# Fixed order of the first loads, and a new order of all other work, in a planned adaLN + linear attention + SwiGLU kernel

## Chip, cores and metric

The kernel runs on one core of one Trainium2 chip. The metric is device time in microseconds (us), as the median of several executions. One execution is also taken by the hardware profiler; the span is the time from its first to its last instruction.

The engines are called PE (matmuls; PEld is its weight load), DVE (vector), ACT (activations), POOL (GpSimd) and SP, which here only issues DMAs.

## The reference

The input x has 2048 tokens of 512 values in bf16. A row `c` gives six modulation vectors. Then come an attention block with feature maps (32 heads of 16), and a gated feed-forward block of width 1376:

```python
mod = (silu(c) @ w_mod).reshape(1, 6, 1, -1)        # sa, ca, ga, sb, cb, gb
h = layernorm(x) * (1 + ca) + sa
x = x + ga * A(h)
h = layernorm(x) * (1 + cb) + sb
x = x + gb * ((silu(h @ w_gate) * (h @ w_up)) @ w_down)

def A(h):                                           # per head
    q, k, v = split(h @ wqkv)
    phi(t) = concat(softmax(t @ w_phi), softmax(-t @ w_phi))
    kv = phi(k).T @ v ;  z = sum over tokens of phi(k)
    return (phi(q) @ kv / (phi(q) @ z + 1e-6)) @ wo
```

## The kernel before

**Tiles and stages.** The 2048 tokens are 16 tiles of 128, in four chunks (`x_ch`, 512 tokens each). The stages are these:

- The first norm: `bn_stats` (L345), `bn_aggr` (L346), the reciprocal root on ACT (L374, L375) or POOL (L378, L379), the negated product with the mean (L381), and normalization to `xn` (L389 on DVE, L393 on ACT, L395 on POOL).
- The modulation: `silu(c)` as a column, then 8 columns of `w_mod` times it for each of 4 row blocks k (L468). Scale and shift of the first norm go to `modA` (L473, L474).
- The fold of `w_phi` into the key and query weights. The 128-row blocks of the weights are transposed (key weights on PE, L515 and L519; query weights by DMA, L292), multiplied with a block-diagonal `BD` made from `w_phi` (L495, L498), by L526, and written back (L529 on ACT, L530 on DVE).
- The turn of `xn` into `hT` (features on partitions). Chunk 0 and the start of chunk 1 go through PE (L558, L411), and ACT or DVE evacuate them with scale and shift (L565, L567, L419, L422). Later tiles go through DMA transposes (L579) with L589 on ACT or L591 on POOL.
- For every tile a key product (L622), exponentials of both signs (L633), their sums S (L639), reciprocals (L643, L644), a value product (L626) scaled into `va` (L649), and the sum over tokens in `kv_ps` (L662). Query tiles do the like with L685, L689, L693 to L700 and a DMA transpose `pT` (L704).
- Attention outputs: L805, reciprocal `A` (L808), `o` (L809), turned by DMA into `oT` (L828) or on PE (L824), projected with `wo` (L838), added to x (L841). `wo` has been scaled by the gate before, on POOL (L761).
- The second norm and the feed-forward block: L890 and L930 (gate and up), L897 to L906, L962 (down), L973, L977, and the stores (L982).

**What sets the order.** Every piece of work is recorded as an `Op` with its alternatives (the engines that could do it and their planned durations), what it reads and what it writes. A list `ORDER`, written out in the file (L47 to L86), then names the operations one by one: `x // 4` is the number of the operation, `x % 4` the chosen alternative. `Plan.run` goes through it and gives each operation a planned start, from the engine's planned free time, the planned ends of what it reads, and the planned landing of DMAs. The instructions are issued in the order of the planned starts. So `ORDER`, and also the planned durations and the constant `DMA`, decide how instructions stand in each engine's queue; the engines then run their queues in order.

```python
            if o.eng == "XBAR" and o.kb > 0:
                dma = max(dma, o.start + self.DMA[0]) + o.kb * 1024 / self.DMA[1]
                o.end = max(o.end, dma + self.DMA[2])
```

**Loads.** All loads are issued by SP (`later`, L289), and the transposes by DMA as well (`transposed`, L292; L579, L704, L828, L852, L942). The row `c` alone comes through ACT's queue. The second argument of `Buf(at=...)` is a planned time before which a buffer counts as not there (`bc` is the row `c`).

**Fill.** Where the plan leaves PE idle, `fill` (its matmul is L1029) puts matmuls on a tile of ones in front of the operation that comes next, by the length of the planned gap, up to 90 us.

Of the kernel before, what the change touches and what calls it, by code (L numbers as in the profile page):

```python
# [35 lines left out]
def fm_size(m):  # L36
# [7 lines left out]


ORDER = [
    20, 44, 0, 48, 8, 56, 4, 64, 148, 12, 52, 264, 272, 116, 164, 24, 268, 276, 16, 168, 280, 172, 76, 176, 68, 181, 284, 290, 80, 72, 152, 294, 60,  # L47
    100, 120, 132, 136, 196, 200, 184, 156, 32, 84, 105, 88, 94, 124, 108, 189, 160, 140, 312, 98, 204, 144, 194, 320, 208, 240, 212, 113, 296, 36,
    28, 245, 316, 128, 324, 304, 248, 216, 228, 548, 224, 301, 329, 233, 364, 480, 332, 376, 252, 220, 464, 420, 236, 308, 472, 512, 424, 338, 257,
    468, 432, 756, 261, 40, 368, 552, 456, 760, 428, 484, 437, 342, 476, 372, 516, 520, 460, 400, 440, 388, 380, 444, 792, 588, 556, 384, 489, 404,  # L50
    592, 452, 448, 392, 852, 860, 800, 492, 408, 502, 524, 344, 396, 628, 498, 354, 816, 856, 506, 358, 560, 529, 808, 536, 636, 532, 565, 584, 724,
    362, 804, 412, 416, 660, 544, 820, 728, 928, 796, 732, 632, 812, 600, 572, 540, 350, 596, 1064, 764, 624, 668, 956, 568, 824, 768, 605, 1072,
    960, 510, 580, 932, 964, 828, 664, 576, 773, 838, 608, 612, 968, 640, 780, 833, 1300, 644, 1068, 845, 1276, 1316, 616, 992, 996, 620, 864, 841,
    784, 869, 848, 648, 776, 938, 972, 950, 1280, 946, 941, 1004, 892, 1009, 976, 788, 872, 888, 900, 876, 1012, 984, 1000, 1160, 896, 980, 988,
    1076, 1200, 952, 1164, 880, 1304, 1016, 904, 884, 736, 1204, 909, 1240, 1172, 1285, 1024, 652, 1177, 912, 916, 1244, 1298, 1212, 1028, 1324,
    1248, 1168, 1332, 1208, 921, 740, 1184, 1289, 924, 1196, 1180, 1294, 1217, 1328, 656, 1020, 1189, 1192, 1312, 1220, 744, 1232, 1492, 1236, 692,
    1252, 1320, 1257, 1260, 748, 1272, 1496, 1224, 1229, 1336, 1264, 1341, 1344, 1268, 1572, 1576, 1356, 1080, 1532, 1084, 1504, 1360, 1536, 1509,
    1512, 1348, 1584, 1544, 1612, 1616, 1500, 1516, 1589, 1524, 1528, 1624, 1353, 1308, 696, 1549, 1580, 1540, 1556, 1592, 1521, 1596, 1629, 1561,
    1652, 700, 1620, 1604, 1568, 1601, 752, 1608, 1636, 1552, 1641, 1396, 1564, 1632, 1644, 1088, 1788, 1648, 1400, 1796, 1780, 1800, 1128, 1136,
    1404, 704, 1804, 1808, 1716, 1656, 1828, 672, 1832, 1784, 1660, 1032, 1724, 1836, 1748, 1840, 1408, 2288, 1428, 2292, 708, 2296, 1792, 712, 716,  # L60
    1720, 1412, 1844, 1848, 1092, 1040, 676, 1852, 1856, 1860, 1036, 2300, 1436, 1752, 1044, 1132, 2452, 680, 2456, 720, 684, 1864, 1048, 2460,
    1756, 1052, 1684, 1460, 1432, 1468, 1056, 1096, 2304, 1464, 1869, 1104, 1880, 1872, 1364, 688, 2308, 1884, 1060, 1816, 1877, 2312, 2136, 2140,
    2316, 1692, 1100, 1368, 1944, 2320, 1416, 2144, 1892, 1108, 1112, 1688, 1372, 1888, 2326, 1924, 1932, 1928, 2148, 1908, 2328, 2440, 1116, 1140,
    1916, 2444, 1912, 1144, 1936, 2152, 1948, 2448, 1984, 1120, 1920, 1940, 2156, 1148, 2346, 1896, 1988, 1960, 1952, 2341, 1900, 1964, 1992, 2160,
    2164, 1996, 1124, 2334, 1824, 2337, 2168, 2174, 1956, 2000, 1376, 2348, 1420, 2404, 2464, 2400, 1472, 2352, 2692, 2004, 2380, 2408, 1904, 1968,
    2008, 2388, 2356, 2176, 2492, 1152, 2364, 1380, 2012, 2412, 2368, 2372, 2016, 2496, 2468, 1476, 2020, 2025, 1384, 2500, 2384, 2189, 1156, 1424,
    1480, 2036, 1388, 2696, 2360, 2182, 2504, 2193, 2376, 1972, 2186, 2392, 2028, 2700, 1392, 2416, 2508, 2396, 2472, 2040, 2704, 2196, 2032, 2248,
    2252, 2228, 1664, 2708, 2476, 2712, 2256, 2044, 2480, 2236, 1440, 1484, 2484, 2490, 2096, 2956, 2200, 2100, 2204, 2960, 1668, 2716, 1672, 1444,
    2048, 2420, 2424, 1448, 1676, 2052, 2964, 1696, 1452, 2104, 2232, 1488, 2944, 2513, 2948, 2260, 2240, 2212, 2744, 2428, 2076, 2516, 2080, 1680,
    1456, 2952, 3208, 2720, 1976, 2244, 2748, 1760, 2526, 2968, 2752, 1700, 2084, 3212, 1704, 1708, 1764, 3216, 2108, 2521, 2533, 2529, 2756, 2216,  # L70
    2724, 2088, 2536, 1768, 1772, 2540, 2060, 2760, 2092, 3196, 1728, 2612, 3200, 2576, 1732, 2068, 2728, 3204, 2064, 2220, 2732, 2996, 2056, 1736,
    3448, 2584, 2628, 2208, 2765, 2224, 2972, 2620, 2072, 2556, 3452, 1776, 2736, 2742, 3000, 3456, 3712, 2976, 2608, 1712, 2264, 3004, 3220, 1740,
    2616, 2980, 3008, 3716, 3248, 2984, 3012, 3720, 3252, 3460, 2636, 2988, 3224, 3256, 2564, 2268, 3017, 2993, 2272, 2572, 2624, 2544, 2768, 3464,
    3228, 2548, 1744, 2774, 2786, 3468, 3260, 2780, 2777, 2560, 3264, 3700, 3232, 2788, 2792, 3020, 2796, 2580, 2568, 3472, 3704, 3236, 2592, 3708,
    3034, 2112, 3026, 3030, 3724, 3240, 3269, 3037, 2800, 2596, 3245, 2600, 3040, 3044, 3476, 3480, 2116, 3048, 3484, 3488, 2120, 2588, 3272, 2276,
    3500, 3052, 2552, 3504, 3492, 1980, 3728, 2124, 2860, 2432, 3290, 3752, 3508, 3732, 3278, 3512, 2808, 3736, 3281, 2604, 3516, 3740, 3496, 3756,
    2632, 3285, 3760, 3292, 2816, 3744, 3521, 3056, 3764, 3768, 3749, 3296, 2644, 2640, 2844, 2812, 2820, 3773, 3524, 2648, 3776, 3542, 2652, 2824,
    2852, 2864, 3530, 3533, 2804, 2656, 3537, 2281, 3794, 2832, 2872, 3544, 3786, 3548, 2848, 3060, 2668, 2672, 2856, 3789, 3552, 2284, 2868, 3782,
    3068, 3796, 2676, 3800, 2828, 3064, 2876, 3804, 3808, 3300, 2836, 2840, 3812, 2884, 2680, 3072, 2880, 2888, 2892, 3304, 3832, 2896, 3836, 2661,
    2436, 3872, 3844, 3880, 2900, 3840, 3308, 2920, 2685, 2904, 3816, 3824, 3848, 2924, 2928, 3820, 3852, 3828, 3888, 3896, 2932, 2688, 3928, 2908,  # L80
    3868, 3892, 2912, 3856, 3876, 2937, 3116, 3860, 3884, 3864, 3900, 3556, 2940, 3076, 3932, 3936, 3124, 3112, 3084, 2128, 3120, 3132, 3140, 3128,
    3136, 3080, 3088, 3092, 3940, 3144, 3096, 3100, 3332, 3172, 3148, 3104, 3108, 3176, 3180, 3152, 3156, 3184, 3340, 3620, 1812, 3384, 3328, 2664,
    3616, 3904, 3628, 3560, 3624, 3160, 2132, 3945, 3312, 3189, 3908, 2916, 3336, 3320, 3632, 3912, 3192, 3344, 3165, 3316, 3364, 3916, 3920, 3348,
    3372, 3368, 3352, 3376, 3324, 3400, 3584, 3356, 3360, 3948, 3424, 3392, 3388, 3380, 3396, 3404, 3428, 3924, 3408, 3412, 3592, 3564, 3432, 3580,
    3436, 3588, 3600, 3168, 1821, 3568, 3572, 3608, 3640, 3636, 3596, 3604, 3440, 3576, 3652, 3644, 3444, 3676, 3612, 3416, 3420, 3648, 3656, 3660,
    3664, 3680, 3669, 3684, 3688, 3693, 3672, 3696, 3952, 3956, 3960, 3964, 3968,  # L86
]


# [32 lines left out]
class Plan:  # L122
# [1 line left out]

    HOP = {"PE": 0.24, "DVE": 0.2, "ACT": 0.2, "POOL": 0.14, "SP": 0.0, "XBAR": 0.08, "NONE": 0.0}
    OWN = {"PE": 0.0, "DVE": 0.19, "ACT": 0.19, "POOL": 0.12, "SP": 0.0, "XBAR": 0.0, "NONE": 0.0}
    DMA = (1.9, 385e3, 0.5, 0.7, 1.3, 1.0)
    LANES = 8

    def __init__(self, slots):  # L130
# [37 lines left out]
    def run(self, fill):  # L168
# [3 lines left out]
        for x in ORDER:  # L172
# [16 lines left out]
# [3 lines that stand above are left out]
            elif o.eng == "XBAR" and o.kb == 0:  # L192
                dma = max(dma, o.end + 0.1) + self.DMA[4 if o.alt[1] > 1.32 else 3]
                o.end = max(o.end, dma + self.DMA[5])
            elif o.kb < 0:
# [13 lines left out]
def kernel(  # L209
# [125 lines left out]
    bwo = [Buf() for _ in range(KD)]  # L335
    bwd = [Buf() for _ in range(FM)]
    bwgu = [Buf(), Buf()]
    bc, bphi = Buf(at=2.75), Buf()
    bWq2 = [Buf() for _ in range(KD)]
    bWk2 = [Buf() for _ in range(KD)]  # L340

# [727 lines left out]
```

## Time and profile before

| what | value |
|---|---|
| median of 5 runs | 202.76 us |
| lowest, highest | 202.27, 203.21 us |
| time of the profiled execution | 202.27 us |
| its span | 200.5 us |
| mean granted TensorE clock | 0.997 |
| PE, DVE, ACT, POOL busy | 193.7, 137.3, 110.1, 125.1 us |

Busy time is the union of an engine's instructions, and its share is of the span. PE's instructions overlap in its pipeline, and its busy time counts the fill as well. 24 matmuls of the kernel are fill. A line in the fences below that begins with a time is a group of like instructions that follow one another: start, length, engine, line, operation, tiles written and read. Square brackets give the idle time of that engine just before, and what ended it.

### The profile page before, as it was taken

The page shows a single profiled execution, that of the slowest core. Times are in us where ns is not written, and L with a number is a line of the kernel's source. Part 1 is how long each engine was busy: PE and PEld are TensorE (multiplying, and loading weights), DVE is VectorE, ACT ScalarE, POOL GpSimd, SP SyncE. Part 2 cuts the span into 40 slices and gives each one's busy share as a digit, 9 for nine tenths or more (in the row PEclk, how much of TensorE's full clock was granted, in tenths as well). Part 3 has the DMA queues.
Part 4 walks back from the last instruction along what each step waited for, and adds up shares of the span by engine and source line. Part 5 has one row for each costly group of instructions (what it writes and reads, how often), then busy time and mean ns, then how long its engine had stood idle before and what let it go on. Part 6 is the DMA issues. An engine that isn't in the chain of part 4 may idle for free.

```text
span 200.5 us, 4670 instructions
## 1 busy us (share of the span) xinstructions
PE 193.7 (97%) x1767; PEld 131.4 (66%) x1767; DVE 137.3 (68%) x277; ACT 110.1 (55%) x244; POOL 125.1 (62%) x211
## 2 busy tenths in 40 slices
PE   7799999999999989999999999999999999999993
PEld 2474555555564767788876767678668867686852
DVE  5979999999989989999988839523314314122343
ACT  2589999998679973571635444562413431341310
POOL 3473999999998997889795758472016260440510
PEclk9999999999999999999999999999999999999998
DMA  5997997989633663949767551721001002010012
GB/s 170 342 351 163 247 310 183 300 157 355 219 56 72 128 97 78 118 94 148 147 129 136 105 105 52 77 70 37 18 26 54 3 7 86 12 56 0 0 56 67
DMA packets 51081, 24.22 MB, mean 121 GB/s; under 512 B 42257, under 2 KB 47858, under 8 KB 51058
## 3 DMA queue, kind: packets, MB, share of 16 engines
q1 hardware_dynamic: 50912, 23.85, 51.6%
q8 instruction: 14, 0.23, 0.5%
q10 hardware_dynamic: 146, 0.07, 0.1%
q14 instruction: 9, 0.07, 0.1%
HBM read 11.58 MB, written 2.10 MB: 68 GB/s over the span
## 4 chain that ended last, share of the span: by engine, by line
PE 84%; ACT 6%; DMA 5%; DVE 2%; SPq 1%; issue 1%; ACTq 0%; DVEq 0%
PE one_ps L890 34%; PE one_ps L962 18%; PE one_ps L626 7%; PE one_ps L838 6%; PE one_ps L622 5%; PE one_ps L685 5%; DMA wmod_sb<-in_w_mod_dram 3%; ACT eq L689 3%; PE one_ps L930 3%; PE kv_ps L662 2%; DMA oT<-o 2%; PE kv_ps L805 2%; PE one_ps L717 1%; PE one_ps L526 1%; SPq L289 1%; ACT hT L565 1%
## 5 line engine op out<-in xcount | busy, mean ns | idle before, releaser
L890 PE MATMUL one_ps<-hT,wgu_sb 128*128 128x256 bf16 (+1 forms) x800 | 76.9, 251 | 0.0
L890 PEld LDWEIGHTS <-wgu_sb 128*128 128x128 bf16 x800 | 65.6, 98 | 10.7
L897 ACT ACTIVATE sg<-one_ps 128x512 bf16<-128x512 f32 (+1 forms) x42 | 23.2, 575 | 39.5 <-PE one_ps L890 32.9
L962 PE MATMUL one_ps<-wd_sb,gu 128*128 128x512 bf16 (+2 forms) x176 | 40.9, 372 | 0.0
L906 POOL TENSOR_TENSOR gu<-usb,sg 128x512 bf16<-128x512 bf16 x16 | 18.4, 1153 | 32.2 <-ACT sg L897 24.5
L900 DVE TENSOR_TENSOR gu<-one_ps,sg 128x512 bf16<-128x512 f32 (+1 forms) x26 | 16.5, 640 | 29.5 <-PE one_ps L890 23.1
L962 PEld LDWEIGHTS <-gu 128*128 128x128 bf16 (+1 forms) x187 | 18.1, 98 | 15.3
L973 DVE TENSOR_TENSOR fg<-one_ps,gab 128x512 bf16<-128x512 f32 (+1 forms) x16 | 10.6, 668 | 15.8 <-PE one_ps L962 15.8
L345 DVE BATCH_NORM_STATS2 st<-x_c 128x6 f32<-128x512 bf16 x32 | 21.1, 677 | 0.3
L639 DVE TENSOR_REDUCE S<-e 128x64 f32<-128x1024 bf16 x16 | 19.3, 1203 | 0.9 <-ACT e L633 0.7
L693 DVE TENSOR_REDUCE Sq<-eq 128x64 f32<-128x1024 bf16 x16 | 19.2, 1202 | 0.0
L904 ACT CAST usb<-one_ps 128x512 bf16<-128x512 f32 x16 | 9.3, 583 | 17.0 <-PE one_ps L890 16.1
L689 ACT ACTIVATE eq<-one_ps 128x512 bf16<-128x512 f32 x32 | 16.7, 612 | 2.1 <-PE one_ps L685 2.1
L633 ACT ACTIVATE e<-one_ps 128x512 bf16<-128x512 f32 x32 | 17.0, 613 | 0.6 <-PE one_ps L622 0.6
L700 POOL TENSOR_TENSOR eq<-eq,Rq 128x512 bf16<-128x512 bf16 x16 | 16.8, 1056 | 0.5
L656 POOL TENSOR_TENSOR e<-e,S 128x512 bf16<-128x512 bf16 x16 | 16.8, 1053 | 0.3
L838 PE MATMUL one_ps<-wo_sb,oT 128*128 128x512 bf16 x64 | 16.3, 379 | 0.5 <-DMA oT<-o 0.5
L626 PE MATMUL one_ps<-wv,hT 128*128 128x512 bf16 x64 | 15.7, 379 | 0.2 <-ACT e L633 0.2
L622 PE MATMUL one_ps<-wk,hT 128*128 128x512 bf16 x64 | 15.8, 379 | 0.0
L685 PE MATMUL one_ps<-wq,hT 128*128 128x512 bf16 x64 | 15.6, 379 | 0.0
L841 DVE TENSOR_TENSOR x_c<-x_c,one_ps 128x512 bf16<-128x512 bf16 x16 | 10.8, 674 | 5.3 <-PE one_ps L838 5.2
L977 POOL TENSOR_TENSOR ot<-x_c,fg 128x512 bf16<-128x512 bf16 x7 | 8.1, 1169 | 6.3 <-DVE fg L973 6.3
(113 smaller groups left out, 268.2 us busy)
## 6 DMA issues: line engine op xcount, KB each, us to landing
wmod_sb<-in_w_mod_dram SPq DMA_DIRECT2D x2, 1024.0 KB, 7.0
out_dram<-ot SPq DMA_DIRECT2D x15, 128.0 KB, 1.9
x_c<-in_A_x_dram SPq DMA_DIRECT2D x3, 512.0 KB, 4.3
wgu_sb<-in_B_w_gate_dram SPq DMA_DIRECT2D x1, 1376.0 KB, 6.3
wgu_sb<-in_B_w_up_dram SPq DMA_DIRECT2D x1, 1376.0 KB, 10.4
wd_sb<-in_B_w_down_dram SPq DMA_DIRECT2D x1, 1280.0 KB, 7.6
wmod_sb<-in_w_mod_dram SPq DMA_DIRECT2D x2, 512.0 KB, 7.2
x_c<-in_A_x_dram SPq DMA_DIRECT2D x2, 256.0 KB, 5.2
```

Of the source, the lines that this page charges most:

```text
L345: pl.op("DVE", r=reads, w=[st6], us=0.6, fn=lambda: nc.vector.bn_stats(st6()[:], src))
L622: nc.tensor.matmul(pk()[:], lhsT=hT[c_i][k][:, cols], rhs=Wk2[:, k, :], start=(k == 0), stop=(k == KD - 1))
L626: nc.tensor.matmul(v()[:], lhsT=hT[c_i][k][:, cols], rhs=wv_sb[:, k, :], start=(k == 0), stop=(k == KD - 1))
L639: pl.op("DVE", r=[e], w=[Ss], us=1.14, fn=lambda: nc.vector.tensor_reduce(Ss()[:].rearrange("p g s h -> p (g s h)"), e()[:].rearrange("p g ...
L685: nc.tensor.matmul(pq()[:], lhsT=hT[c_i][k][:, cols], rhs=Wq2[:, k, :], start=(k == 0), stop=(k == KD - 1))
L689: pl.op("ACT", r=[pq, btab], w=[be[sg]], us=0.48, fn=lambda sg=sg: nc.scalar.activation(eq[:, :, sg].rearrange("p g h f -> p g (h f)"), pq ...
L693: pl.op("DVE", r=be, w=[Sq], us=1.14, fn=lambda: nc.vector.tensor_reduce(Sq()[:].rearrange("p g s h -> p (g s h)"), eq[:].rearrange("p g s ...
L838: nc.tensor.matmul(a()[:], lhsT=oT()[:, j0 + j, :], rhs=wo_sb[:, j, :], start=(j == 0), stop=(j == KD - 1))
L890: nc.tensor.matmul(ps_()[0:fsz, q * n:(q + 1) * n], lhsT=wgu_sb[:, k, i, m * P:m * P + fsz], rhs=h2[k], start=(k == 0), stop=(k == KD - 1))
L897: pl.op("ACT", r=[g, btab], w=[sg], us=0.08 + 0.41 * L / CW, fn=lambda: nc.scalar.activation(sg()[0:fsz, 0:L], g()[0:fsz, 0:L], ACT.Silu))
L906: pl.op("POOL", r=[usb, sg], w=[gu], us=0.17 + 0.98 * L / CW, fn=lambda: nc.gpsimd.tensor_tensor(gu()[0:fsz, 0:L], usb()[0:fsz, 0:L], sg() ...
L962: nc.tensor.matmul(fp()[:], lhsT=b()[0:fsz, c0:c0 + P], rhs=wd_[0:fsz, m, wcs], start=(m == 0), stop=(m == FM - 1))
```

## The change

`ORDER` is replaced as a whole. Two constants of the plan change with it. The recorded operations, their alternatives, and what each computes are the same.

```diff
 ORDER = [
-    20, 44, 0, 48, 8, 56, 4, 64, 148, 12, 52, 264, 272, 116, 164, 24, 268, 276, 16, 168, 280, 172, 76, 176, 68, 181, 284, 290, 80, 72, 152, 294, 60,
-    100, 120, 132, 136, 196, 200, 184, 156, 32, 84, 105, 88, 94, 124, 108, 189, 160, 140, 312, 98, 204, 144, 194, 320, 208, 240, 212, 113, 296, 36,
+    0, 4, 8, 44, 64, 48, 52, 132, 116, 12, 56, 68, 76, 72, 172, 80, 164, 136, 176, 16, 60, 148, 100, 120, 168, 196, 200, 124, 85, 152, 180, 140,
+    156, 88, 105, 92, 184, 108, 204, 190, 208, 128, 98, 216, 20, 240, 161, 228, 212, 264, 144, 225, 194, 112, 220, 420, 272, 244, 268, 32, 276, 24,
...
-    DMA = (1.9, 385e3, 0.5, 0.7, 1.3, 1.0)
+    DMA = (1.7, 385e3, 0.5, 0.7, 1.3, 1.0)
...
-    bc, bphi = Buf(at=2.75), Buf()
+    bc, bphi = Buf(at=3.0), Buf()
```

In `ORDER`, 0 is the load of chunk 0 of x, 4 the key weights, 8 `w_phi`, 12 and 16 the two row halves of the first third of `w_mod`, 20 and 24 the two halves of chunk 1, 28 the value weights, 32 the query weights, 36 and 40 chunks 2 and 3. The queue of SP, as it is built from the two lists:

| place | before | after |
|---|---|---|
| 1 | chunk 1, first half | chunk 0 |
| 2 | chunk 0 | key weights |
| 3 | w_phi | w_phi |
| 4 | key weights | w_mod, half |
| 5 | w_mod, half | w_mod, half |
| 6 | chunk 1, second half | chunk 1, one half |
| 7 | w_mod, half | query weights |
| 8 | query weights | chunk 1, other half |
| 9 | chunk 2 | value weights |
| 10 | value weights | chunk 2 |

Of the alternatives, the new list takes ACT for two L565 more, three L861 more, one L589 more, two L653 more and three L393 fewer; POOL for three L395 more, one L977 more, and one L591, two L652, two L863 and one L915 fewer; DVE for two L567, one L859 and one L977 fewer and one L915 more. The number of fill matmuls goes from 24 to 22, and of their columns from 10,706 to 10,060.

## The prediction

> **What bounds the kernel now.** I read the page first (engine shares, chain), then the chain in order of time, then busy time by stretch, then the timelines of the stretches that decide. From the page:
>
> ```profile
> span 200.5 us, 4670 instructions
> PE 193.7 (97%) x1767; PEld 131.4 (66%) x1767; DVE 137.3 (68%) x277; ACT 110.1 (55%) x244; POOL 125.1 (62%) x211
> DVE  5979999999989989999988839523314314122343
> PE 84%; ACT 6%; DMA 5%; DVE 2%; SPq 1%; issue 1%; ACTq 0%; DVEq 0%
> ```
>
> PE looks like the only bound, but the DVE row is 9 or near it in the first 22 slices (about 5 us each). Busy time by stretch (columns: stretch, length, then PE, PEld, DVE, ACT, POOL busy) says how near:
>
> ```profile
> 4.24:13.59 9.35, 7.96 (x117) 5.29 (x115) 7.89 (x24) 6.04 (x15) 4.74 (x7) 1.00 1.00 347
> 13.59:17.87 4.28, 4.11 (x26) 2.06 (x25) 3.90 (x15) 3.68 (x10) 2.47 (x4) 1.00 0.79 147
> 17.87:71.61 53.74, 53.65 (x487) 30.23 (x487) 52.33 (x87) 49.78 (x124) 49.65 (x83) 1.00 0.79 201
> 71.61:200.50 128.89, 125.23 (x1134) 92.77 (x1131) 70.99 (x145) 49.16 (x96) 66.63 (x105) 1.00 0.37 69
> ```
>
> Between the first sum of exponentials (S, L639, at 17.87) and the attention outputs around 71.6, DVE is busy 52.33 of 53.74 us: it binds beside PE there. After 71.6 DVE has room and PE alone sets the end. So what the change saves at the start reaches the end only if both PE and DVE come earlier to about 72 us. The start is set by loads; the chain in order of time:
>
> ```profile
> 2.59 6.73 DMA wmod_sb<-in_w_mod_dram
> 9.36 0.55 PE one_ps L468 x16
> 10.37 0.91 PE one_ps L526 x16
> 11.30 1.00 ACT wk L529 x2
> 12.34 0.81 ACT hT L565 x2
> ```
>
> PE waits for the first half of w_mod, then folds the key weights (L526). The same stretch in the timeline shows the second half as the later gate:
>
> ```profile
> 11.42 0.47 PEld L468 LDWEIGHTS <-wmod_sb 128*128 128x128 bf16 x16 [0.28 <-DMA wmod_sb<-in_w_mod_dram]
> 12.02 0.16 DVE L473 COPY modA<-one_ps 128x4 f32<-128x4 f32 x1 [0.71 <-PE one_ps L468]
> 13.59 1.07 PE L622 MATMUL one_ps<-wk,hT 128*128 128x512 bf16 x4
> 17.87 1.22 DVE L639 TENSOR_REDUCE S<-e 128x64 f32<-128x1024 bf16 x1 [0.38 <-ACT e L633]
> ```
>
> The reader is to see that modA (the scale and shift of the first norm) waits 0.71 us for PE, which has just got its w_mod data, and that the first key product (L622) starts at 13.59. At the far end of the DVE-bound stretch stands one more wait:
>
> ```profile
> 72.51 0.82 PE L838 MATMUL one_ps<-wo_sb,oT 128*128 128x512 bf16 x3 [0.53 <-DMA oT<-o]
> ```
>
> **The change part by part: loads.** In the semaphore events of the trace the loads land at: first half of chunk 1 4.22, chunk 0 5.52, w_phi 5.72, key weights 7.33, w_mod half 9.32, second half of chunk 1 10.0, w_mod half 11.38, query weights 12.8, chunk 2 14.2, value weights 16.2. They land in the order of issue, so a load's landing goes by the KB ahead of it with its own: 256, 768, 784, 1296, 1808, 2064, 2576, 3088, 3600, 4112. SP's new order is chunk 0, key weights, w_phi, both w_mod halves, half of chunk 1, query weights, the other half, value weights, chunk 2. (So the query weights still part the halves of chunk 1.) The sums are 512, 1024, 1040, 1552, 2064, 2320, 2832, 3088, 3600, 4112. Read between the old points: chunk 0 4.9 (was 5.5), key weights 6.5 (7.3), w_phi 6.5 (5.7), w_mod 8.3 and **10.0** (9.3, 11.38), chunk 1 10.7 and 12.8 (4.2, 10.0), value weights 14.2 (16.2), chunk 2 16.2 (14.2). The gain that counts is 1.38 us at w_mod. The Trainium skill ("DMA: Bandwidth & Descriptors", Anatomy of one DMA) has about 2.0 us plus bytes over 436e3 per us; the 524 KB that leave the way would then save 1.20, and w_mod's second half would have landed at 0.72 + 2.0 + 6.05 = 8.8 instead of the 11.38 of the trace. The trace decides: 1.38. With the rule the sum below is 0.2 worse.
>
> **First key product.** PE at 10.0: 16 L468 (0.55), then by the built order three tiles' transposes (L558, 0.22 each) with fill matmuls of 1,008, 1,334 and 220 columns between (0.42 + 0.56 + 0.09): L622 at 10.0 + 0.55 + 0.66 + 1.07 = 12.3, against 13.59: 1.3 us. What it needs is there: key-weight transposes 6.5 to 7.6, the L526 group behind the first L468 group at 8.9 to 10.0, ACT's three casts (0.48 apart) to 10.9, modA 0.6 + 0.25 after L468's start at 10.85, hT pairs on ACT (0.345 a piece) from 10.9. Moved behind this point: the eight L411 transposes of chunk 1 (0.45) and some fill (two matmuls fewer in all, but 1,264 columns more behind L622: 0.53, standing where PE is meant to wait). PE's own room is 1.3 - 0.45 = 0.8 us, plus the oT wait of 0.53.
>
> **DVE.** From modA at 10.85 to the first S, DVE's new order has 4 statistics (L345, 0.60 from start to start), 6 L567 (0.25), 2 L346 (0.09), one L381 (0.06): 4.15, so S at 15.0; ACT's first exponential, behind eight hT pieces (10.9 + 2.76) and its own 1.1, allows 14.9. That is 2.8 us earlier than 17.87. But work has moved behind S: counting DVE's instructions from S to the same fifth attention output (94 instead of 87): 3 L345, 3 L346, one L381 and two L422 (0.28) more, two L567 fewer: 1.80 + 0.26 + 0.06 + 0.56 - 0.50 = 2.2. Net on DVE: 2.8 - 2.2 = **0.6 us**. The Trainium skill ("Perfetto Trace Analysis", Identifying the Most-Contended Engine) says matmul busy time misleads and to take the engine with the highest occupancy in each regime. Here it speaks against the change: PE at 97% would give 1.3, DVE's rows give 0.6. I take 0.6, since 52.33 of 53.74 leaves DVE no place to absorb more.
>
> **The oT wait.** The first oT transpose, of the same size, landed 2.4 us after its issue; this one, issued at 68.62, took 3.85. In the trace's DMA packets, a 16 KB packet of the instruction queue (page: q8, 14 packets) holds one DMA engine from 69.6 for 1.4 us. By PE's order that fetch comes five matmuls earlier against its neighbours in the new kernel, about 0.5 us. Bounds: 0.5 gained, or 0.5 lost if another transfer is hit; I take 0.2 gained.
>
> **The rest.** Later loads on SP trade places: the two other w_mod parts with a transpose between, w_down ahead of gate, w_o behind it. w_o landed at 35 and is wanted by POOL's L761 at 56.3: even behind gate (landed at 41.8, 5 us for its size) it has about 10 us of cover, and if that were gone the four L761 (1.15 us each) and the output products behind them would slip. POOL has three L395 more (0.77), and fewer L591, L652, L863, L915; ACT three L393 fewer, two L565, three L861 more: within 1 us each, on engines with 4 us of slack in the long stretch. The tail has the same PE work. Unknown: plus or minus 0.5.
>
> **Sum.** 0.6 + 0.2 = 0.8 us. The profiled execution was 202.27 with a span of 200.5 (1.8 around it), 0.5 below the median 202.76 of the five; the saving is taken from the median: **202.0 us**.
>
> **The rivals.**
> - *Given back in the middle.* PE gets more fill where it is meant to wait, and DVE starts its statistics at 4.9, not 4.24. If idle time on DVE grows by 0.4 and the oT wait stays, 0.2 is left: 202.5. For: ACT has ten L565 instead of eight ahead of the exponentials. Against: DVE idles already 1.4 in the stretch. Chance 0.24.
> - *The start is kept whole.* If PE alone bound, 1.3 and part of the 0.53 wait come out: about 1.5, 201.3. Against: DVE's stretch. Chance 0.18.
> - *Slower: chunk 1 late.* In DVE's queue its statistics stand ahead of L567, the second half of the first tile's hT. If chunk 1 lands after 10.85, each us of delay is one on DVE, PE and ACT behind it. There is 0.15 of room by bytes; with the longest issue-to-landing of an x load (8.9, from issue near 3.6) it lands at 12.5, costs 1.65, and 1.65 - 0.8 = 0.85 is lost: 203.6. It decides against the kernel from a landing at 11.65, by over 0.3% from 12.3. Chance 0.12.
> - *The change does not do what it says.* SP's built order does move the loads; only loads landing out of issue order could undo it, and none did so before. It would end as the 202.5 case and is counted there.
>
> **How the numbers follow.** Forecast case 0.46 (202.0), with 0.42 of it past the bound. A measurement of this kernel tells about 0.3%, 0.6 us, from no change. Faster: 0.42 + 0.18 + 0.02 of the given-back case = 0.62. Same: 0.04 + 0.22 = 0.26. Slower: 0.12. The range 201.1 to 203.0 leaves out the slower case and a third of the kept one.
>
> **What would show it.** Right: w_mod's second half at 10.0, modA at 10.85, L622 at 12.3, S at 15.0, the fifth attention output (71.61) about 0.6 earlier, L838's wait under 0.53. Wrong: modA before 10.5 or after 11.3; DVE waiting for x_c; S early but the attention outputs not; or a gain that appears only behind 72 us.

## The result, and the profile after

The changed kernel takes 201.79 us (median of 31 runs), against 203.08 us for the kernel before on the same chips (52 runs). The ratio is 0.9943, with a 95% interval of 0.9927 to 0.9958: 0.57% faster, or 1.15 us (0.85 to 1.48). It is the quotient of the means of the fast runs, which leave out those more than 1.5% above the fastest of their kernel, and so not that of the two medians. The profiled execution spans 199.6 us instead of 200.5. The prediction had 0.8 us.

The page after has the same shape as the page before. These are its span, engine row, DVE slices (40 equal slices of the span) and chain:

```profile
span 199.6 us, 4657 instructions
PE 194.1 (97%) x1765; PEld 132.2 (66%) x1765; DVE 136.8 (69%) x274; ACT 111.5 (56%) x249; POOL 124.4 (62%) x209
DVE  5898999999899999998997896332041404434143
PE 85%; DMA 5%; ACT 5%; DVE 3%; SPq 1%; issue 0%; DVEq 0%; ACTq 0%
```

The span is 0.9 us shorter while PE is busy 0.4 us longer, so no PE work went away. The difference is in when the work starts. The timeline of the start after the change (start, length, engine, line, operation, tiles; idle time just before in brackets):

```profile
9.51 0.55 PE L468 MATMUL one_ps<-silucT,wmod_sb 128*128 128x1 bf16 x16
10.10 0.16 DVE L473 COPY modA<-one_ps 128x4 f32<-128x4 f32 x1
11.68 1.03 PE L622 MATMUL one_ps<-wk,hT 128*128 128x512 bf16 x4
15.11 1.22 DVE L639 TENSOR_REDUCE S<-e 128x64 f32<-128x1024 bf16 x1
71.89 0.82 PE L838 MATMUL one_ps<-wo_sb,oT 128*128 128x512 bf16 x3 [0.23 <-DMA oT<-o]
```

`modA` has no wait in front of it now and comes 1.9 us earlier (10.10, was 12.02). So does the first key product (11.68, was 13.59). The first S is 2.8 us earlier (15.11, was 17.87). The output product L838 at 72 us waits 0.23 us where it waited 0.53.

The chain in order of time (start, length, what) still begins with w_mod and still passes through the `oT` transpose:

```profile
2.19 5.94 DMA wmod_sb<-in_w_mod_dram
9.01 1.38 ACT wk L529 x3
15.77 1.96 ACT e L633 x4
68.32 3.52 DMA oT<-o
71.89 1.04 PE one_ps L838 x4
```

Of PE's waits, before:

```profile
PE one_ps L838 <- DMA oT<-o: 0.5, 1, 0.5
PE one_ps L468 <- DMA wmod_sb<-in_w_mod_dram: 0.5, 1, 0.5
PE one_ps L626 <- ACT e L633: 0.2, 1, 0.2
```

and after, where the one for w_mod is gone (as are 0.5 for the key weights and 0.3 for w_phi) and the one for ACT's exponentials has grown:

```profile
PE one_ps L626 <- ACT e L633: 0.6, 1, 0.6
PE one_ps L838 <- DMA oT<-o: 0.2, 1, 0.2
```

**The balance on PE.** Take every PE matmul of the trace from the first key product to the last one. Count as useful the median step from its start to the next start for its kind, as waiting what a step takes beyond that, and the fill's steps as fill.

| | before | after | difference |
|---|---|---|---|
| first L622 starts | 13.59 | 11.68 | -1.91 |
| useful steps behind it | 181.32 | 181.77 | +0.45 |
| fill behind it | 0.56 | 1.09 | +0.53 |
| waits behind it | 1.63 | 1.74 | +0.11 |
| last matmul starts | 197.10 | 196.28 | -0.82 |

The 0.45 is the eight L411 transposes that moved behind the first key product. The first four rows add up to the last; the span itself is 0.85 shorter. What the table can't say is which of them counts: whether the start carries to the end, whether DVE limits that, and whether the fill costs anything. The experiments ask this.

### The profile page after: what moved, and what is told of

Same layout as the page of the kernel before. It is cut to its first block, busy times and chain, and to the rows that moved or that the text cites. A ratio compares the mean times of both kernels' runs of the same rounds, so it can differ in the third digit from the quotient of the medians.

```text
span 199.6 us, 4657 instructions
## 1 busy us (share of the span) xinstructions
PE 194.1 (97%) x1765; PEld 132.2 (66%) x1765; DVE 136.8 (69%) x274; ACT 111.5 (56%) x249; POOL 124.4 (62%) x209
## 4 chain that ended last, share of the span: by engine, by line
PE 85%; DMA 5%; ACT 5%; DVE 3%; SPq 1%; issue 0%; DVEq 0%; ACTq 0%
PE one_ps L890 33%; PE one_ps L962 19%; PE one_ps L626 7%; PE one_ps L838 7%; PE one_ps L685 6%; PE one_ps L622 5%; DMA wmod_sb<-in_w_mod_dram 3%; PE one_ps L930 3%; PE kv_ps L662 2%; DMA oT<-o 2%; PE kv_ps L805 2%; ACT e L633 1%; ACT hT L565 1%; ACT eq L689 1%; DVE st L345 1%; PE one_ps L717 1%
## 5 line engine op out<-in xcount | busy, mean ns | idle before, releaser
L890 PE MATMUL one_ps<-hT,wgu_sb 128*128 128x256 bf16 (+1 forms) x800 | 75.4, 251 | 0.0
L962 PE MATMUL one_ps<-wd_sb,gu 128*128 128x512 bf16 (+2 forms) x176 | 40.4, 372 | 0.0
L973 DVE TENSOR_TENSOR fg<-one_ps,gab 128x512 bf16<-128x512 f32 (+1 forms) x16 | 10.5, 668 | 24.2 <-PE one_ps L962 23.4
L838 PE MATMUL one_ps<-wo_sb,oT 128*128 128x512 bf16 x64 | 15.8, 379 | 0.2 <-DMA oT<-o 0.2
L622 PE MATMUL one_ps<-wk,hT 128*128 128x512 bf16 x64 | 15.8, 379 | 0.0
L393 ACT ACTIVATE xn<-x_c,ln_nmr,ln_rstd 128x512 bf16<-128x512 bf16 x10 | 8.1, 810 | 9.8 <-POOL ln_nmr L359 9.7
```

The source lines that it names most:

```text
L622: nc.tensor.matmul(pk()[:], lhsT=hT[c_i][k][:, cols], rhs=Wk2[:, k, :], start=(k == 0), stop=(k == KD - 1))
L838: nc.tensor.matmul(a()[:], lhsT=oT()[:, j0 + j, :], rhs=wo_sb[:, j, :], start=(j == 0), stop=(j == KD - 1))
L890: nc.tensor.matmul(ps_()[0:fsz, q * n:(q + 1) * n], lhsT=wgu_sb[:, k, i, m * P:m * P + fsz], rhs=h2[k], start=(k == 0), stop=(k == KD - 1))
L962: nc.tensor.matmul(fp()[:], lhsT=b()[0:fsz, c0:c0 + P], rhs=wd_[0:fsz, m, wcs], start=(m == 0), stop=(m == FM - 1))
```

## The experiments

Ratios are to the kernel before, as is the changed kernel's 0.9943.

### Is it the place of w_mod in the queue? (e1)

The changed kernel, with SP's order `x0, wk, w_phi, w_mod half, chunk 1 half, chunk 1 half, w_mod half, wq, wv, chunk 2`; all other work stays.

```diff
+        [setattr(o, "alt", a) for o, a in zip(sorted(self.ops[:10], key=lambda o: o.start), [self.ops[n].alt for n in (0, 1, 2, 3, 5, 6, 4, 8, 7, 9)])]
```

> The changed kernel with one thing altered in SP's queue: both halves of chunk 1 go ahead of w_mod's second half (512 KB more in front of it); every compute engine's queue is untouched. By the KB in front, that half of w_mod lands near 11.0 instead of 9.5. Theory A (the start's gain reaches the end through the DVE-bound stretch): modA 1.5 us later, first S about 1.2 later, the whole 0.7 to 1.3 us slower than the changed kernel. Rival B (the gain comes from the new order behind 20 us, the start is absorbed): 0.2 us slower at most.

Measured: ratio 1.0022 (0.9993 to 1.0051), 0.8% or about 1.6 us above the changed kernel, where 0.7 to 1.3 was expected. PE's wait for w_mod in this run:

```profile
PE one_ps L468 <- DMA wmod_sb<-in_w_mod_dram: 1.1, 1, 1.1
```

`modA` comes at 11.11 and the first key product at 12.68, both 1.0 later than in the changed kernel, and the last matmul ends 1.3 later. So the place of w_mod's second half is worth as much as the whole gain, and what is late at the start is late at the end. (The query weights, too, stand one place further back in e1; no wait of PE in this run is for them.) The KB ahead of a load may not settle its landing: w_mod's second half has the same 2,576 KB to its end as in the old order, and lands at 10.47, where it landed at 11.08 to 11.38 in the three traces with the old order of loads (before, e2, e8). But e1 is one trace, and the list at the end shows how far the landing of one load scatters.

### The loads or the order of work, each alone (e2, e4)

e2 is the changed kernel with the old order of loads. e4 is the kernel before with the new order of loads. The edit is the line above with the lists `(5, 0, 2, 1, 3, 6, 4, 8, 9, 7)` and `(0, 1, 2, 3, 4, 5, 8, 6, 7, 9)`.

> The changed kernel with SP's first ten loads in the order of the kernel before; every compute engine's queue is untouched. w_mod's second half near 11.4, chunk 0 near 5.5, value weights near 16.2 where PE wants them at 14.5. Theory A: 1.2 to 2.0 us slower than the changed kernel, so slower than the kernel before. Rival B: within 0.3 us of the changed kernel, still faster than before.

> The kernel before with SP's first ten loads in the new order; compute queues untouched. DVE's first two statistics are of chunk 1, which lands near 10.2 instead of 4.2, and everything on DVE stands behind them. Theory A with queues: modA near 15, 3 us late, and the whole 2 to 3 us slower than before. If the load order alone made the gain: 0.5 to 1 us faster than before.

Measured: e2 1.0088 (1.006 to 1.0117), e4 1.0289 (1.0212 to 1.0365). Each half of the change alone is slower than the kernel before, by 1.8 and 5.9 us. e2 is 2.9 us above the changed kernel, and 1.2 to 2.0 was expected. Waits of PE and of DVE in e2:

```profile
PE one_ps L515 <- DMA wk<-in_A_wqkv_dram: 1.2, 1, 1.2
DVE st L345 <- DMA x_c<-in_A_x_dram: 1.3, 1, 1.3
```

and the head of DVE's timeline in e4:

```profile
10.52 1.88 DVE L345 BATCH_NORM_STATS2 st<-x_c 128x6 f32<-128x512 bf16 x3 [6.36 <-DMA x_c<-in_A_x_dram]
```

In the old work order DVE's next statistics are those of chunk 1. With the new loads this chunk lands at 10.5, and the statistics of chunk 0, which has been there since 4.2, stand behind it. The first key product moves from 13.59 to 19.84 (+6.25) and the last matmul from 197.37 to 203.49 (+6.12). e4 was expected to lose less, since the whole length of an in-order queue's wait had not been counted.

A part of both losses is the TensorE clock, which no expectation had. The granted clock by slice (40 slices, tenths of full speed), of e2 and then of e4:

```profile
PEclk9979999999999999999999999999999999999999
PEclk9967999999999999999999999999999999999999
```

In e2 it was 0.50 from 9.73 to 13.14 us. There the 16 fold matmuls (L526) took 1.80 us instead of 1.05, and the first key product came 2.88 us behind the start of the second L468 group instead of 2.17. So about 0.7 of its delay of 2.45 against the changed kernel is the clock, and the rest the load. In e4 the clock was 0.50 from 11.56 to 18.39, where PE waited for most of the time and was busy for 3.1 us. Without the clock e2 still loses: in its six executions with a mean clock of at least 0.997 the median was 204.7 us, against 202.4 for the kernel before.

### Only the two places of the queue that differ by w_mod (e3)

The kernel before, with w_mod's second half in place 6 and chunk 1's second half in place 7: the list `(5, 0, 2, 1, 3, 4, 6, 8, 9, 7)`.

> The kernel before with places 6 and 7 of SP's queue exchanged: w_mod's second half ahead of chunk 1's second half; compute queues untouched. w_mod's half lands near 10.7 instead of 11.4, the half of chunk 1 near 11.4 instead of 10.0. If w_mod's landing alone made the gain: 0.4 to 0.7 us faster than before. Theory A with queues: DVE has its statistics of that half ahead of modA, so modA comes at 11.4 + 1.3 = 12.7 instead of 12.0, and the kernel is 0.3 to 0.7 us slower than before.

Measured: 1.0002 (0.9968 to 1.0035). The interval leaves room for 0.6 us either way, so the time tells neither a gain nor the expected loss of 0.3 to 0.7 from none. In the trace `modA` is not earlier but later (12.55, was 12.02), and the span is 0.5 longer. PE has the first of these two waits anew, and DVE the second:

```profile
PE one_ps L468 <- DVE ln_nmr L381: 0.3, 1, 0.3
```

```profile
DVE st L345 <- DMA x_c<-in_A_x_dram: 1.5, 2, 1.2
```

In the work order of before, DVE reaches chunk 1's statistics ahead of what PE needs, so an earlier w_mod is worth nothing there. Between the first key product and the last matmul's end lie 183.78 us in e3, 183.78 in the kernel before and 183.65 in e4: in these three the part behind the first key product keeps its length, wherever it starts. It is not fixed for good: it is 184.96 in e8 below, with the same work order, and 184.87 to 185.74 in the changed kernel, e1, e2 and e11, which share the new one.

### Which engine binds behind the start? (e5, e6)

The changed kernel with about 1.0 us more on PE (ten matmuls on ones), or 1.13 us more on DVE (a second sum of exponentials), both in key tile 8, so at one place of the stretch.

```diff
+            for _ in range(10 if i == 8 else 0): nc.tensor.matmul(kv_ps[:, 0, :].rearrange("p (g n) -> p g n", n=P)[:, :, NDW:P], lhsT=ones[:, 0:P], rhs=ones[:, 0:4 * (P - NDW)].rearrange("p (g n) -> p g n", g=4), start=False, stop=True, skip_group_check=True)
```

```diff
+            d, e()[:].rearrange("p g s h f -> p (g s h) f"), axis=AX.X, op=ALU.add) for d in [Ss()[:].rearrange("p g s h -> p (g s h)")] + [probe[:]] * (i == 8)])
```

> The changed kernel with ten more fill matmuls of 240 columns (1.0 us of PE) in the key product of tile 8, in the middle of the stretch in which DVE and PE are both busy. If PE binds up to 72 us: 0.8 to 1.0 us slower than the changed kernel. If DVE binds (prediction's sum): 0.2 to 0.5 slower, the rest hidden.

> The changed kernel with one more sum of exponentials on DVE (1.13 us from start to start, into an unused tile) behind that of tile 8. If DVE binds up to 72 us (prediction's sum): 0.9 to 1.1 us slower than the changed kernel. If PE binds: 0.2 to 0.5 slower.

Measured: e5 1.0002 (0.9986 to 1.0018), about 1.2 us above the changed kernel, give or take 0.5: all of it arrives. e6 0.9961 (0.9942 to 0.998), about 0.4 us above, and its interval overlaps with the changed kernel's. From the first S to the last sum over tokens (L662), busy time by stretch (stretch, length, PE, PEld, DVE, ACT, POOL) of the changed kernel is

```profile
15.11:55.54 40.43, 39.84 (x339) 21.42 (x338) 39.24 (x64) 37.94 (x105) 37.20 (x64) 1.00 0.88 225
```

and that of e6

```profile
15.39:56.15 40.76, 40.17 (x339) 21.26 (x338) 40.08 (x65) 38.38 (x105) 37.18 (x64) 1.00 0.90 222
```

The stretch is 0.33 longer; the rest of the 1.13 went into DVE's idle time (1.19 before, 0.68 now) and into closer overlap of its instructions. Measured from tile 8's key product to that last L662, e5 is 1.03 longer and e6 0.32. So PE binds behind this place; DVE at 97% is close, but some 70% of the extra work still disappears.

### What does the added fill cost? (e7)

```diff
-FILL_FROM, FILL_TO, FILL = 1.3, 90.0, 0.85
+FILL_FROM, FILL_TO, FILL = 1.3, 14.0, 0.85
```

> The changed kernel without the fill matmuls that stand behind the first key product (five, 2,016 columns, 0.84 us of PE between 50 and 70 us). If PE binds there: 0.3 to 0.8 us faster than the changed kernel. If DVE and the transposes bind: no change within 0.2 us, with PE waits in the fill's place.

Measured: 0.9943 (0.9922 to 0.9965), no change. PE's waits now include these:

```profile
PE one_ps L838 <- ACT sg L897: 0.5, 1, 0.5
PE one_ps L411 <- ACT xn L393: 0.3, 1, 0.3
```

The L411 at 65.2 us stands where fill was, and PE waits there instead. The L838 at 71.70 is the wait for `oT`, which landed at 71.65; the profile puts it down to ACT here, and it is 0.46 instead of 0.23. From the first key product to the start of the last matmul it is 184.78 us in e7 and 184.60 in the changed kernel, though 1.09 us of fill are gone. So the fill behind the first key product costs nothing that can be measured, and its growth of 0.53 in the balance marks time in which PE has to wait in this order anyway, most of it between 64 and 68 us.

### The instruction fetch and the transposes (e8, e11)

Both cut the early fill into smaller matmuls (256 columns in the kernel before, 192 in the changed one), so that PE's instructions are fetched at another time. The DMA packets of the trace show this fetch as packets of 16 KB, 14 in the kernel, one for about 250 instructions of PE. The edit of e11 is shown; that of e8 has `CW // 2` for 192.

```diff
-                fns.append(lambda n=min(left, CW): f(n))
-                left -= CW
+                fns.append(lambda n=min(left, 192): f(n))
+                left -= 192
```

> The kernel before with its early fill in matmuls of 256 columns instead of 512: the same columns, 18 more weight loads and matmuls before 13.6 us, so that each 16 KB instruction fetch of PE comes 36 instructions sooner, the one at 69.6 us about 2 us sooner and ahead of the oT transpose. If the fetch held up that transpose: it lands near 71.0, L838's wait of 0.53 goes, 0.3 to 0.5 us faster than before, unless the fetch meets another transfer. If not: oT still takes 3.8 us and the time is the same.

> The changed kernel with its early fill of the same columns cut into matmuls of 192 columns: about 48 more PE instructions ahead of 60 us, so that PE's 16 KB instruction fetch (69.12, and 1.15 us long, in the changed kernel) comes at about 66.5 to 67.5. Fetch theory: the transposes oT land 2.4 us after issue instead of 3.5, L838's wait of 0.4 goes, and the whole is 0.2 to 0.4 us faster than the changed kernel (0.992 to 0.993 of before). Rival, as the like run on the kernel before showed: the fetch now holds up a pT transpose issued just ahead of it, L805 waits in L838's place, nothing is gained (0.993 to 0.997).

Measured: e8 1.0033 (1.0013 to 1.0053), e11 0.9969 (0.9916 to 1.0022). Neither shows a gain; e8 loses. In both the wait on `oT` is gone and one on `pT` has come. PE's timeline of e8, then of e11:

```profile
71.85 0.43 PE L805 MATMUL kv_ps<-KVZ,pT 128*128 128x68 bf16 x8 [0.67 <-DMA pT<-eq]
```

```profile
71.16 0.43 PE L805 MATMUL kv_ps<-KVZ,pT 128*128 128x68 bf16 x8 [0.88 <-DMA pT<-eq]
```

The fetch moved less than expected in e11 (68.61, against 69.12 in the changed kernel and an expectation of 66.5 to 67.5). The `pT` transpose issued at 66.25 took 4.9 us, where the median of its kind in that stretch is 3.2; the `oT` issued at 68.1 took 3.4. In e8 likewise a `pT` took 4.8 us and the `oT` 3.25 instead of 3.84. In e8 the fetch did not move as expected: it came at 69.80, where 69.60 had been and about 67.6 was expected. In all four traces the late transpose is one in flight at a fetch. Not every transpose in flight at one is late, though; the list at the end has the count over all traces. At the two places where the fetch stood in e8 and e11, the rival of e11 was right: a `pT` was late instead of the `oT`.

### Taking work off ACT at the start (e9, e10)

In the changed kernel ACT stands idle 0.63 us ahead of an L565, and the wait ends with DVE's L567, which reads the same `one_ps` tile:

```profile
13.29 0.81 ACT L565 ACTIVATE hT<-one_ps,modA 128x128 bf16<-128x128 bf16 x2 [0.63 <-DVE hT L567]
```

ACT's exponentials are then late, and this is the 0.6 that PE waits. e9 moves that pair of L565 to DVE, e10 the next tile's pair too.

```diff
+        [setattr(self.ops[n], "alt", self.ops[n].alts[1]) for n in (59,)]
```

> The changed kernel with the two L565 of hT (second tile, halves 2 and 3) moved from ACT to DVE, right behind DVE's own two L567 of that tile; every other queue unchanged. In the changed kernel's trace ACT idles 0.63 us ahead of these two, because both engines read the same bank of one_ps and the second waits for the first; ACT is then late with e (L633), and PE waits 0.75 for it at 17.0. PE theory (PE binds from the first key product on; the two runs that added 1 us to PE and to DVE speak for it): ACT's first exponential starts about 1.0 us earlier, PE's wait at 17 falls from 0.75 to under 0.3, and the whole is 0.3 to 0.7 us faster than the changed kernel: 0.991 to 0.993 of before. DVE theory: DVE has 0.5 us more work ahead of the first S, the fifth attention output comes 0.2 to 0.5 later, the whole 0.995 to 0.997 of before. Third: the time won at 17 is lost again at the next wait (oT, L838, or the attention chain at 60 to 72): same as the changed kernel, 0.994.

> As the run before, and the L565 pair of the third tile goes to DVE too: 0.5 us more on DVE, 0.7 us less on ACT. PE theory: the exponentials come earlier again, but PE's wait at 17 is already mostly gone, so 0 to 0.2 us more than the run before (0.990 to 0.993 of before). DVE theory: DVE is 1.0 us over the changed kernel ahead of S, S comes later than 15.1 by 0.3 to 0.6, and PE then waits for DVE in place of ACT: 0.995 to 1.000.

Measured: 0.9974 (0.9925 to 1.0023) and 0.9969 (0.9915 to 1.0023): these intervals (six executions each) are too wide to tell either from the changed kernel or to choose between the theories. The traces tell more. In e9 ACT's first exponential starts 1.06 us behind the first key product instead of 2.31, as expected, and PE's wait for it is gone. The next lines of e9 show who is late instead:

```profile
16.04 0.15 DVE L381 TENSOR_REDUCE ln_nmr<-ln_mv 128x2 f32<-128x4 f32 x1
16.22 0.81 ACT L565 ACTIVATE hT<-one_ps,modA 128x128 bf16<-128x128 bf16 x2 [1.07 <-DVE ln_nmr L381]
16.30 1.52 POOL L395 TENSOR_SCALAR xn<-x_c,ln_mv,ln_nmr 128x512 bf16<-128x512 bf16 x2 [1.13 <-DVE ln_nmr L381]
```

and in e10 it reaches PE in full:

```profile
17.05 0.62 PE L411 MATMUL one_ps<-ident_b,xn 128*128 128x128 bf16 x8 [0.67 <-POOL xn L395]
```

The negated mean (L381) stands behind the added L567 in DVE's queue, POOL's normalization behind that, and PE's transposes behind POOL. From the first key product to the last matmul's end it is 185.03 us in e9 and 185.65 in e10, against 184.87. So ahead of the first S, DVE's order does reach PE. The DVE theory of e10 had PE wait for DVE in ACT's place; the way by POOL stood in no expectation. No experiment showed a version better than the changed kernel.

## Why the prediction was right, and where its steps were not

**The loads: right in kind, too small.** The prediction had w_mod's second half at 10.0; it landed at 9.47. Most of the landings that it read off the KB were too late: chunk 0 at 4.01 (predicted 4.9), key weights 5.98 (6.5), w_phi 6.17 (6.5), the first half of w_mod 8.12 (8.3), chunk 1's halves 10.16 and about 12.3 (10.7 and 12.8), value weights 13.83 (14.2); only chunk 2 came at its 16.2. A good part of this is in the first landing: 512 KB of chunk 0 in first place are there at 4.01, 0.2 earlier than the 256 KB of half of chunk 1 were in its place, and the scale by KB had its origin in that old first load. The estimate from the Trainium skill ("DMA: Bandwidth & Descriptors", Anatomy of one DMA) gave a saving of 1.20 us at w_mod; the trace shows 1.91. That section states its figures for single transfers that GpSimd issues; these loads are issued by SP and stand one behind the other.

**`modA` and the first key product: right chain, 0.6 too late.** `modA` came at 10.10 (predicted 10.85), L622 at 11.68 (12.3). `modA` before 10.5 was one of the prediction's own signs of being wrong. The 1.58 us between the two is the same as before (1.57). S came at 15.11, predicted 15.0, but this agreement is luck: from `modA` to S it took 5.01 us, not 4.15, and that made up for the early `modA`. (The bound that it gave for ACT there, 14.9, adds up to 14.8, which changes nothing.)

**The DVE step: this is the one that failed.** The prediction took DVE's net gain of 0.6 as the one that counts, "since 52.33 of 53.74 leaves DVE no place to absorb more". Its counting was right: by stretch, DVE has 2.0 us more work between S and the fifth attention output than before, for 2.2 counted.

```profile
4.24:11.68 7.44, 7.35 (x105) 5.20 (x104) 6.21 (x20) 4.82 (x12) 3.22 (x5) 1.00 1.04 336
11.68:15.11 3.43, 3.43 (x22) 1.68 (x20) 3.28 (x12) 2.80 (x8) 1.59 (x3) 1.00 1.59 314
15.11:71.30 56.19, 55.52 (x508) 31.67 (x507) 54.35 (x94) 52.27 (x133) 50.28 (x84) 1.00 0.79 196
71.30:199.60 128.30, 125.02 (x1130) 92.71 (x1127) 70.94 (x143) 50.14 (x98) 67.67 (x107) 1.00 0.34 69
```

But neither the size nor the conclusion held. The fifth attention output came 0.31 earlier, not 0.6. DVE's timelines, before and after:

```profile
71.61 0.63 DVE L809 TENSOR_TENSOR o<-kv_ps,A 128x512 bf16<-128x512 f32 x1
71.30 0.63 DVE L809 TENSOR_TENSOR o<-kv_ps,A 128x512 bf16<-128x512 f32 x1
```

S was 2.76 earlier, the work took 2.02 of this, and DVE's idle time in the stretch grew from 1.41 to 1.84: a further 0.43, for which the sum had no term. And DVE had room: e6 put 1.13 us more on it in that stretch and 0.3 came out, while e5 put 1.0 on PE and 1.2 came out. PE binds, as its own share of the same row (53.65 of 53.74) said. The prediction had the Trainium skill's rule on occupancy ("Perfetto Trace Analysis", Identifying the Most-Contended Engine) speak for DVE, because matmul busy time misleads. That section says that matmul busy time is no good measure of how close PE is to its roofline, and to judge PE's headroom by MFU and the busy share of the weight loads. By that share (30.23 of 53.74 before) PE had headroom; e5 shows that here it had none for more work.

**The right sum is PE's.** The start gives -1.91, the moved L411 +0.45, fill and waits +0.64: -0.82 in the trace. The prediction had the first two terms in its passage on PE's room (1.3 less 0.45), and not the third. So its 0.8 met the profiled span's 0.9 partly by luck: a start mis-sized by 0.6 and waits not counted, of 0.64. The timed 1.15 us lies a little above both (see below). One trace is one execution. In six further kernels with the same work ahead of it, the first key product started at 11.31 to 11.95 in five, and at 13.00 in one (e9), where the loads came late.

**The `oT` wait: right in size.** 0.2 gained was predicted; PE's row shows 0.3 (0.53 to 0.23). The fetch came 0.5 us earlier on the clock (69.60 to 69.12), but only 0.2 earlier against the issue of the `oT` (0.98 behind it before, 0.80 after), where 0.5 was forecast; the transpose landed in 3.52 instead of 3.84. And 2.4 us, from which the prediction took the transpose to be late, is the time of the first `oT` alone, in all thirteen traces; the six after this one in the changed kernel took 3.05 to 3.38. So the fetch can account for only a part of the 3.84.

**The rest at plus or minus 0.5.** The new wait of PE for ACT's exponentials at 17 us (0.2 to 0.6) is the given-back rival in small, through ACT, as its argument said. Its condition on DVE, 0.4 more idle time, was met as well (0.43); its other one, that the `oT` wait stays, was not.

**The rivals.** The case of the start kept whole had the right mechanism, with PE alone binding; its 1.5 us was too much because the L411 and the added waits were left out. Chunk 1 late did not happen: its first half landed at 10.16 and DVE waits for no chunk. Its mechanism is real all the same: it is most of what makes e4 6 us slower, with the old order of DVE's work.

**What stays open.** The ratio's 1.15 us is 0.3 above the trace's 0.82. A part of this goes with the granted clock. Of the 137 executions of the kernel before that have a clock on record, 24 had a mean under 0.994, and a median of 204.2 us; those of at least 0.997 had 202.5. Of 32 executions of the changed kernel, one was under 0.994. A stretch like the one in e2, 3.41 us at 0.50, would cost 1.7 us, by an estimate from these two figures. Without the executions under 0.997, e7, which timed 0.9943 like the changed kernel, is 0.9 us below the kernel before in the same batch. Why the clock falls stays open, as no trace has the kernel before with a low mean. Ahead of its first key product PE stands idle for 1.39 of 9.35 us, in the changed kernel for 0.09 of 7.44; whether this is the reason was not tried.

## What to carry to other kernels

When loads set the start, order them by what the first product of the bound engine needs last, and reorder the in-order queues of the other engines with them: here either half alone was slower than the kernel before, and both together were faster. A second engine that is 97% busy beside the bound one need not be a bound; add a microsecond to each and see which one arrives. And when a wait is taken from one queue, look for what stands behind the work that takes its place: ACT's relief went to DVE, from there to POOL, and back to PE.

## What the runs showed of the hardware

- A 16 KB packet of the instruction queue held one DMA engine for 1.0 to 1.4 us near 69 us in four traces (before, after, e8, e11). Between 57 and 125 us of all thirteen traces, the 82 `pT` transposes that met no such packet took 4.0 us at most (79 of them 3.0 to 3.6). Of the 53 that met one, 22 took 4.1 to 5.3 us and 31 took 3.0 to 3.8. So a packet goes with every `pT` over 4.1 us, but not every packet delays one; what decides is not known.
- In first place, the 512 KB of chunk 0 landed at 4.01 to 4.23 us in nine traces, no later than the 256 KB of half of chunk 1 in four (4.22 to 4.39).
- In seven traces with the same start of work (the changed kernel, e5, e6, e7, e9, e10, e11), the landing of w_mod's second half ranged from 8.87 to 9.74, with one at 10.79 (e9), and the first key product moved with it, from 11.31 to 11.95, and to 13.00 in e9.
- The granted clock fell to 0.50 for 3.41 us in e2 (mean 0.992) and for 6.83 us in e4 (mean 0.982), both at the start of the kernel.
